# Two token blocks at once in the second of two MLPs behind bucketed attention, and more attention tiles transposed by DMA

## The chip, the cores and the metric

One core of one Trainium2 chip. The metric is the device time of one execution in microseconds (us), as the median of several runs; lower is better.

## The reference

```python
q_bucket, k_bucket = bits of (q @ proj > 0), (k @ proj > 0)      # 6 bits: 64 buckets
scores = where(q_bucket == k_bucket, q @ k.T / 8, -1e9)
attn = softmax(scores) @ v            # 2 batches, 8 heads, 768 tokens, 64 columns
x = attn as 1536 tokens x 512
g = s * relu(x @ w1_in) ** 2 + b;     y = g @ w1_out             # 512 -> 2048 -> 512
h = y @ w2_in; g = h * clip(h + 3, 0, 6) / 6; out = g @ w2_out   # 512 -> 2048 -> 512
```

All inputs are float32 and the output is float32.

## The kernel before, in words

**Tokens.** The 1536 tokens are four blocks ("units") of 384: two per batch. In attention a unit has four pairs of heads, so there are 16 pairs g, and a pair has six slots: two heads by three tiles of 128 queries. A slot is: scores `S` (128 queries by 768 keys, four matmuls, `qk`, L466), the maximum (`smax`, L475), exp with the row sum (`sexp`, L482), a transposition, and after six slots the product with the values (`pv_mm`, L560). The sums' reciprocals are spread over the partitions and multiplied in (`x_scale`, L570), and the result is kept in two fp32r parts, high and low, in X (`x_hi`, `x_lo`). All large matmuls are made of fp32r parts in this way: high x high, high x low, low x high.

**Two ways to transpose.** Pairs g under DMA_FROM (L31) turn a slot with six transposes on TensorE (`turn`, L514) and copy it out of PSUM (`evict`, L519); their product is 24 fp32 matmuls. Pairs from DMA_FROM on split the slot into two fp16 parts (`s_hi` on ScalarE, L493, `s_lo` on VectorE, L498) and transpose it by a DMA from SP's queue (`s_tr`, L508); their values are scaled, split and transposed too (`v_scale` to `v_tr`, L361 to L386), and the product is 36 fp16 matmuls.

**MLPs.** A job (m, j) is MLP m on block j: 32 weight tiles of 128 x 512, the first 16 for `w_in` (a group of 12 matmuls each, 4 row blocks by 3 parts, L648 to L660), the last 16 for `w_out` (four groups accumulate one output tile). After an input group the activation is made in PSUM and split into G (`g_relu` to `g_lo`). When an MLP's weights are met for the first time they come as 64-bit floats (512 KB a tile), are put together as fp32 (`w_exp`, `w_ends`, `w_join`), and stored to a scratch tensor (`w_store`); later jobs fetch the 256 KB tile (`w_fetch`, L628). Each job splits each tile into a high and a low part (`w_hi` L633, `w_lo` L638), on ScalarE, VectorE or GpSimd.

**Room.** X of blocks 2 and 3 is the room of blocks 0 and 1 (L310). PSUM has two score tiles (a third, `Sx`, during the first unit), one bank for the product, and one, later three banks for the MLP groups.

**The order** is not written by hand. Every operation is given to a planner (`Plan`, L37) with its possible engines, cost, due time, needs and buffers; it lays out a list and the kernel is emitted in that order, each engine's queue in order. Due times come from JOBS (L32): per job (m, j, n), where n is the number of attention slots that run beside it. The first unit's 24 slots come first. `gate` (L734) lets a slot start only when the MLP work is near its place, six slots and ten groups ahead at most, and `pull` (L743) lets a group start only when the slots up to six before its place have been begun. Small DMAs go out on SP's or ScalarE's queue as the planner finds room.

Of the kernel before, what the change touches and what calls it, by code (L numbers as in the profile page):

```python
# [19 lines left out]
S = 768  # L20
# [221 lines left out]
def attn_moe_moe2(ctx, tc, qT, kT, vN, vT, cst, w1_in, w1_out, w2_in, w2_out, out):  # L242
# [403 lines left out]
    acc = {}  # L646

    def mm(key, i, j, k):  # L648
        hi, lo = wq[key]["hi"], wq[key]["lo"]
        c = i % 4  # L650
        if i < 16:
            src, k0, nk = X[j], 0, 4
        else:
            src, k0, nk = G[4 * c:4 * c + 4], 4 * c, 16
        if k0 + k == 0:
            acc[key[0]] = ps[ring(("acc", key))].tile([128, 512], F32, tag="mm", name="mm")
        a = acc[key[0]][:, 0:NQ]
        for p, (w, xi) in enumerate(((hi, 0), (hi, 1), (lo, 0))):
            nc.tensor.matmul(out=a, lhsT=w[:, k, :], rhs=src[k][:, xi, :],  # L659
                             start=(k0 + k == 0 and p == 0), stop=(k0 + k == nk - 1 and p == 2))  # L660
        if k == 3:
            acc[key] = a
            del wq[key]
# [3 lines left out]
    def g_relu(m, f, key):  # L667
        h = acc.pop(key)
# [85 lines left out]
    for g in range(NP):  # L754
# [33 lines left out]
        if by_dma(g):  # L788
# [4 lines left out]
            add("TR", t + 8, (1.4, 3.7, 0.3), v_tr, (g,), needs=[("vl", g)], acq=[("v", ("v", g))], gives=[("v", g)], rel=[(("vh", g),)])  # L793
        else:
            add("DMA", t + 4, (0.62, 1.1, 0.8), load_v, (g,), acq=[("v", ("v", g))], gives=[("v", g)])
        for i in range(SPP):
# [10 lines left out]
            if by_dma(g):  # L807
                add("ACT", a + 3.4, 0.8, s_hi, (s,), needs=[("ex", s)], acq=[("P", ("P", s))], gives=[("hi", s)])
                add("DVE", a + 4.3, 0.96, s_lo, (s,), needs=[("hi", s)], gives=[("lo", s)], rel=[(("S", s),)])
                add("TR", a + 5.4, (1.4, 3.7, 0.3), s_tr, (s,), needs=[("lo", s)] + ([("wi", "t", s - 1)] if tq else []), acq=pt,  # L810
# [5 lines left out]
        add("PE", a + 6.0, 3.2 if by_dma(g) else 4.2, pv_mm, (g,), needs=[("pt", SPP * g + i) for i in range(SPP)] + [("v", g)],  # L816
            acq=[("pv", ("pv", g))], gives=[("pv", g)], rel=[(("pt", g, 0),), (("pt", g, 1),), (("v", g),)])
# [8 lines left out]
    def before(k, jn, i):  # L826
        return [(k,) + divmod(32 * jn + i - 1, 32)] if jn + i else []

    for jn, (m, j, n) in enumerate(JOBS):
        t0, dt = M[jn]  # L830
        prev = [("mm", jn - 1, 28 + f // 4) if jn else None for f in range(16)]
        for i in range(32):
            key = (jn, i)
            t = t0 + i * dt
            if jn == first[m]:
                tw = t - 4.0
                add("DMA", tw - 4.0, (0.45, 1.46, 0.8), w_load, (m, i, key), needs=[("pv", 0)] if m == 0 else past(jn, i, AHEAD),
                    acq=[("wr", ("wr", key))], gives=[("wr",) + key])
                add("ACT", tw, 0.68, w_exp, (key,), needs=[("wr",) + key], gives=[("we",) + key])
                add({"ACT": 0.79, "POOL": 0.8, "DVE": 0.46}, tw, 0, w_ends, (key, 0), needs=[("wr",) + key] + before("wi", jn, i),  # L840
                    acq=[("wf", ("wf", key))], gives=[("wd", 0) + key] + [("wi",) + key])
                add("DVE", tw, 0.46, w_ends, (key, 1), needs=[("we",) + key, ("wd", 0) + key], gives=[("wd", 1) + key])
                add("DVE", tw, 0.69, w_join, (key,), needs=[("wd", 1) + key], gives=[("wf",) + key], rel=[(("wr", key),)])
                last = [(("wf", key), 2)]
                add("DMA", tw, (0.45, 0.73, 1.9), w_store, (m, i, key), needs=[("wf",) + key], gives=[("ws", m, i)], rel=last)
            else:
                add("DMA", t - 4.0, (0.45, 0.73, 0.0), w_fetch, (m, i, key), needs=[("ws", m, i)] + past(jn, i, AHEAD) + before("wi", jn, i),
                    acq=[("wf", ("wf", key))], gives=[("wf",) + key, ("wi",) + key])
                last = [(("wf", key),)]
            add({"ACT": 0.62, "DVE": 0.42}, t - 2.0, 0, w_hi, (key,), needs=[("wf",) + key] + before("wh", jn, i), acq=[("wh", ("wh", key))], gives=[("wh",) + key])  # L850
            add({"POOL": 1.3, "DVE": 0.67}, t - 2.0, 0, w_lo, (key,), needs=[("wh",) + key], acq=[("wl", ("wl", key))], gives=[("wl",) + key], rel=last)
            acc_key = ("acc", key if i < 16 else (jn, i - i % 4))
            for k in range(4):
                if i < 16:
                    ins = ("x", j, k) if m == 0 else ("y", j, k)
                else:
                    ins = ("g", jn, 4 * (i % 4) + k)
                head = k == 0 and (i < 16 or i % 4 == 0)
                ins = [ins] + (pull(jn, i) if k == 0 else [])
                add("PE", t + k * dt / 4, MM / 4, mm, (key, i, j, k),  # L860
                    needs=[("wh",) + key, ("wl",) + key] + ins + ([("mk", jn, i, k - 1)] if k else past(jn, i, 1) + (["banks"] if head and (jn or i) else [("R", g) for g in range(4)] if head else [])),
                    acq=[("mm" if jn == 0 and i == 0 else ("mm", "mmx"), acc_key)] if head else [],
                    gives=[("mm", jn, i) if k == 3 else ("mk", jn, i, k)],
                    rel=[(("wh", key),), (("wl", key),)] if k == 3 else [])
            te = t + dt
            if i < 16:
                add("ACT", te, 0.48, g_relu, (m, i, key), needs=[("mm", jn, i)], acq=[("r", ("r", key))], gives=[("gr", jn, i)])
                add("DVE", te + 0.1, 0.6, g_prod, (m, i), needs=[("gr", jn, i)], gives=[("gp", jn, i)], rel=[(("r", key),)])
                add("ACT", te + 0.2, 0.48, g_hi, (m, i), needs=[("gp", jn, i), "G"] + [p for p in prev[i:i + 1] if p],
                    gives=[("gh", jn, i)])  # L870
                add("DVE", te + 0.3, 0.6, g_lo, (m, i), needs=[("gh", jn, i)], gives=[("g", jn, i)], rel=[(acc_key,)])
            elif i % 4 == 3:
                d = (i - 16) // 4
# [80 lines left out]
```

## Time and profile before

| | |
|---|---|
| median of 3 runs | 786.98 us (785.93 to 787.44) |
| profiled execution | 784.16 us |
| its span in the profile | 782.4 us |
| TensorE matmuls busy | 763.2 us, 98% |
| TensorE weight loads, VectorE, ScalarE, GpSimd | 88%, 79%, 60%, 22% |
| mean share of the DMA engines | 66% |

Engines: PE is TensorE's matmuls, PEld its weight loads, DVE VectorE, ACT ScalarE, POOL GpSimd, SP SyncE, whose queue issues most DMAs. In a window's row stand each engine's busy time with its number of instructions, the granted TensorE clock as a share of full speed, the share of the 16 DMA engines and GB/s. A group's row has line, engine, operation, out<-in, shapes, count | busy time, mean ns of one | idle time before it and what ended it. The first matmul of the first MLP starts at 93 us; the jobs' first groups start at 213, 287, 412, 489, 566 and 646 us and so on.

### The profile page before, as it was taken

The numbers are of one execution on the slowest core, as the hardware profiler recorded it, in microseconds if no ns is written. First come the engines' busy times: TensorE is split into PE (matmuls) and PEld (weight loads), VectorE is DVE, ScalarE is ACT, GpSimd is POOL, SyncE is SP. The second block draws the span as 40 slices with busy tenths as digits, with TensorE's granted clock in tenths as the row PEclk, the third lists the DMA queues.
The fourth block names the chain that finished last, engine by engine and source line by source line (L and its number), as shares of the span: only waits on it lengthen the run. The fifth ranks groups of instructions, "written<-read, shape, count | busy, mean of one in ns | idle before, by whom it ended". The sixth has DMA issues, their size and how long they took to land.

```text
span 782.4 us, 13073 instructions
## 1 busy us (share of the span) xinstructions
PE 763.2 (98%) x4620; PEld 688.2 (88%) x4620; DVE 617.8 (79%) x1049; ACT 468.6 (60%) x853; POOL 172.9 (22%) x142
## 2 busy tenths in 40 slices
PE   8888899999999999999999999999999999999998
PEld 4565678989899997877979999999999999999998
DVE  6888788999887679999978866887787758856862
ACT  5777668876575368978867722854377416503710
POOL 4213134332300013452322510521012100001000
PEclk7999999999999999999999999999999999999999
DMA  7378775688644677887998848866785764444441
GB/s 272 97 272 331 267 245 177 207 322 268 224 142 129 234 223 251 263 305 244 338 293 196 252 146 206 225 160 157 187 237 127 200 156 132 124 134 121 132 139 39
DMA packets 105057, 159.93 MB, mean 204 GB/s; under 512 B 50592, under 2 KB 56864, under 8 KB 104992
## 3 DMA queue, kind: packets, MB, share of 16 engines
q1 hardware_dynamic: 104704, 158.89, 66.0%
q8 instruction: 36, 0.59, 0.3%
q14 instruction: 29, 0.24, 0.1%
q10 hardware_dynamic: 288, 0.22, 0.1%
HBM read 115.56 MB, written 32.51 MB: 189 GB/s over the span
## 4 chain that ended last, share of the span: by engine, by line
PE 88%; DVE 4%; ACT 3%; DMA 3%; issue 1%; SPq 0%; DVEq 0%; ACTq 0%
PE mm L659 66%; PE S L471 7%; PE pv L566 7%; PE S L517 5%; DMA wr<-w_in 2%; DVE nx L477 1%; PE S L431 1%; DMA krx<-k_t 1%; ACT P L490 1%; PE S L444 1%; DVE wf L611 1%; PE S L549 0%; DVE K1x L459 0%; DVE wf L620 0%; DVE pt L528 0%
## 5 line engine op out<-in xcount | busy, mean ns | idle before, releaser
L659 PE MATMUL mm<-X,wh 128*128 128x384 f32 x1024 | 264.9, 339 | 0.5 <-DVE G L693 0.4
L659 PE MATMUL mm<-G,wh 128*128 128x384 f32 x1024 | 265.3, 340 | 0.0
L642 POOL TENSOR_TENSOR wl<-wf,wh 128x512 fp32r<-128x512 f32 x84 | 113.5, 1355 | 413.2 <-DVE wh L393 226.4
L659 PEld LDWEIGHTS mm<-X,wh 128*128 128x128 f32 x1024 | 181.5, 188 | 6.7 <-issue 3.7
L659 PEld LDWEIGHTS mm<-G,wh 128*128 128x128 f32 x1024 | 181.7, 188 | 4.6 <-issue 3.3
L659 PE MATMUL mm<-G,wl 128*128 128x384 f32 x512 | 172.4, 337 | 0.0
L659 PE MATMUL mm<-X,wl 128*128 128x384 f32 x512 | 172.0, 336 | 0.0
L642 DVE TENSOR_TENSOR wl<-wf,wh 128x512 fp32r<-128x512 f32 x172 | 120.9, 705 | 12.2 <-ACT wh L390 3.3
L390 ACT ACTIVATE wh<-wf 128x512 fp32r<-128x512 f32 x145 | 90.5, 628 | 47.4 <-PE mm L659 32.5
L477 DVE TENSOR_REDUCE nx<-S 128x1 f32<-128x768 f32 x96 | 90.4, 953 | 21.1 <-PE S L471 20.6
L659 PEld LDWEIGHTS mm<-G,wl 128*128 128x128 f32 x512 | 96.0, 188 | 0.1
L659 PEld LDWEIGHTS mm<-X,wl 128*128 128x128 f32 x512 | 96.1, 188 | 0.0
L393 DVE TENSOR_SCALAR wh<-wf 128x512 fp32r<-128x512 f32 x111 | 47.6, 429 | 52.0 <-PE mm L659 49.2
L490 ACT ACTIVATE P<-S,nx 128x768 f32<-128x768 f32 x72 | 64.7, 901 | 16.4 <-DVE nx L477 15.9
L471 PE MATMUL S<-K,Q 128*128 128x512 f32 (+1 forms) x312 | 69.7, 350 | 1.4 <-DVE pt L528 0.4
L517 PE MATMUL S<-cw,P 128*128 128x128 f32 x432 | 61.0, 281 | 6.9 <-ACT P L490 6.7
L517 PEld LDWEIGHTS S<-cw,P 128*128 128x128 f32 x432 | 51.0, 144 | 15.9 <-ACT P L490 12.1
L471 PEld LDWEIGHTS S<-K,Q 128*128 128x128 f32 x312 | 52.0, 194 | 9.4 <-issue 1.8
L614 POOL TENSOR_SCALAR wf<-wr 128x512 uint16<-128x512 uint16 x36 | 30.9, 857 | 106.6 <-DMA wr<-w_in 29.1
L566 PE MATMUL pv<-pt,v 128*64 128x384 f32 (+1 forms) x384 | 53.4, 429 | 0.1
L620 DVE SCALAR_TENSOR_TENSOR wf<-wr,wf 128x512 int32<-128x512 int32 x64 | 48.1, 755 | 2.4
L611 DVE TENSOR_SCALAR wf<-wr 128x512 uint16<-128x512 uint16 x89 | 46.3, 534 | 4.2 <-ACT wr L602 2.5
(381 smaller groups left out, 820.6 us busy)
## 6 DMA issues: line engine op xcount, KB each, us to landing
wf<-w SPq DMA_DIRECT2D x192, 256.0 KB, 2.7
wr<-w_in SPq DMA_DIRECT2D x32, 512.0 KB, 5.3
w<-wf SPq DMA_DIRECT2D x64, 256.0 KB, 5.5
wr<-w_out SPq DMA_DIRECT2D x32, 512.0 KB, 5.5
K<-ks SPq DMA_DIRECT2D x16, 768.0 KB, 6.6
ks<-K SPq DMA_DIRECT2D x10, 768.0 KB, 7.8
qr<-q_t SPq DMA_DIRECT2D x14, 384.0 KB, 4.4
kr<-k_t SPq DMA_DIRECT2D x6, 768.0 KB, 5.3
```

The costliest lines, as they stand in the source:

```text
L390: nc.scalar.activation(out=out, in_=in_, func=AF.Copy, scale=scale)
L393: e.tensor_scalar(out=out, in0=in_, scalar1=scale, scalar2=None, op0=ALU.mult)
L471: nc.tensor.matmul(out=sp[:, c0:c1], lhsT=queries(g)[a][:, h, 128 * t:128 * t + 128], rhs=keys(g)[a][:, h, c0:c1], start=(a == 0), stop=(a ...
L477: nc.vector.reduce_max(out=nx, in_=sd[s]["sp"][:, 0:S], axis=AX.X, negate=True)
L490: nc.scalar.activation(out=d["p"], in_=d["sp"][:, 0:S], func=AF.Exp, bias=d["nx"], scale=1.0, accum_out=pd[g]["sums"][:, c:c + 1])
L517: nc.tensor.transpose(d["sp"][:, 128 * c:128 * c + 128], d["p"][:, 128 * c:128 * c + 128], ident)
L566: nc.tensor.matmul(out=d["pv"][64 * h:64 * h + 64, 0:NQ], lhsT=d["v"][:, vc, 64 * h:64 * h + 64], rhs=d[h][:, :, pc, :] if by_dma(g) else ...
L611: nc.vector.tensor_scalar(out=f16, in0=r16, scalar1=(13, 0x8000)[half], scalar2=None, op0=(ALU.logical_shift_right, ALU.bitwise_and)[half])
L614: nc.gpsimd.tensor_scalar(out=f16, in0=r16, scalar1=2.0 ** -13, scalar2=2.0 ** -14 - 0.5, op0=ALU.mult, op1=ALU.add)
L620: nc.vector.scalar_tensor_tensor(out=wf, in0=wq[key]["raw"][:, :, 1], scalar=3, in1=wf, op0=ALU.logical_shift_left, op1=ALU.bitwise_or)
L642: e.tensor_tensor(out=lo.rearrange("p a b -> p (a b)"), in0=d["wf"], in1=d["hi"].rearrange("p a b -> p (a b)").bitcast(F32), op=ALU.subtract)
L659: nc.tensor.matmul(out=a, lhsT=w[:, k, :], rhs=src[k][:, xi, :], start=(k0 + k == 0 and p == 0), stop=(k0 + k == nk - 1 and p == 2))
```

## The change

- DMA_FROM goes from 12 to 9: pairs 9, 10 and 11 are transposed by DMA as pairs 12 to 15 are.
- JOBS: the second MLP runs on blocks 0 and 1 together, and on 2 and 3 together. Each of its 32 weight tiles is fetched and split once for two groups, one per block. As G holds 16 tiles, it goes by halves of the features: eight input tiles and eight output tiles for half 0, then half 1. The outputs of half 0 go to a scratch tensor and are fetched and added after half 1.
- Order of jobs: before (MLP, block) 00, 01, 10, 11, 02, 12, 03, 13 with 24, 10, 8, 10, 10, 10, 0, 0 slots; now 00, 01, 1 on 0 and 1, 02, 03, 1 on 2 and 3 with 24, 12, 18, 18, 0, 0 slots.
- X of block 2 gets its own room; block 3 uses that of block 0.
- The product of the first four pairs is emitted in three parts (`PV_PARTS`), the third score tile is used for two more slots (`XT`), and in the first two further groups of a first-MLP job a group's last row block may follow the next groups' first ones (`EASE`).
- The planner's cost of a transposing DMA goes from 3.7 to 2.2 us.

```diff
-WARM, PTX, DMA_FROM = 12, 2, 12
+WARM, PTX, DMA_FROM = 12, 2, 9
+PV_PARTS, EASE = 3, 3
-JOBS = ((0, 0, 24), (0, 1, 10), (1, 0, 8), (1, 1, 10), (0, 2, 10), (1, 2, 10), (0, 3, 0), (1, 3, 0))
+JOBS = ((0, (0,), 24), (0, (1,), 12), (1, (0, 1), 18), (0, (2,), 18), (0, (3,), 0), (1, (2, 3), 0))
...
-        X.append([p.tile([128, 2, NQ], F32R, name=f"X1{k}") for k in range(4)])
-        X.extend(X[0:2])
+        X.extend([p.tile([128, 2, NQ], F32R, name=f"X{u}{k}") for k in range(4)] for u in (1, 2))
+        X.append(X[0])
...
-    def pv_mm(g):
+    def pv_mm(g, part):
         d = pd[g]
-        d["pv"] = ps_v.tile([128, 512], F32, tag="pv", name="pv")
-        for c in range(NC):
+        if part == 0:
+            d["pv"] = ps_v.tile([128, 512], F32, tag="pv", name="pv")
+        n = NC // parts(g)
+        for c in range(n * part, n * part + n):
...
+    oscr = [[dr_p.tile([128, NQ], F32, name=f"o{j}{d}") for d in range(4)] for j in range(4)]
+    def mm(n, k):
+        V, src, j, c0, nk, name = group[n]
+        hi, lo = wq[V]["hi"], wq[V]["lo"]
+        if c0 + k == 0:
+            acc[name] = ps[ring(("acc", name))].tile([128, 512], F32, tag="mm", name="mm")
+        a = acc[name][:, 0:NQ]
         for p, (w, xi) in enumerate(((hi, 0), (hi, 1), (lo, 0))):
+            nc.tensor.matmul(out=a, lhsT=w[:, k, :], rhs=(X[j] if src is None else G[src:])[k][:, xi, :],
+                             start=(c0 + k == 0 and p == 0), stop=(c0 + k == nk - 1 and p == 2))
...
+    def o_keep(j, d):
+        queue[0].dma_start(out=oscr[j][d], in_=od.pop((j, d)))
+    def o_fetch(j, d):
+        od[j, d] = o_tile()
+        queue[0].dma_start(out=od[j, d], in_=oscr[j][d])
+    def o_add(j, d, name):
+        o = od[j, d]
+        nc.vector.scalar_tensor_tensor(out=o, in0=acc.pop(name)[:, 0:NQ], scalar=1.0 / 6.0, in1=o, op0=ALU.mult, op1=ALU.add)
...
+        for x in range(halves):
+            for i in [fs * x + f for f in range(fs)] + [16 + 4 * d + cs * x + c for d in range(4) for c in range(cs)]:
+                for e, j in enumerate(blocks):
...
+                    group.append((len(visits), None if i < 16 else fs * e + 4 * (c - cs * x), j, 0 if i < 16 else 4 * (c - cs * x),
+                                  4 if i < 16 else 4 * cs, name))
...
-    XT = SPU - 4
+    XT = SPU - 2
...
-            add("TR", t + 8, (1.4, 3.7, 0.3), v_tr, (g,), needs=[("vl", g)], acq=[("v", ("v", g))], gives=[("v", g)], rel=[(("vh", g),)])
+            add("TR", t + 8, (1.4, 2.2, 0.0), v_tr, (g,), needs=[("vl", g)], acq=[("v", ("v", g))], gives=[("v", g)], rel=[(("vh", g),)])
...
-        add("ACT", a + 11.0, 0.48, x_hi, (g,), needs=[("xs", g)] + (["G"] if u else []) + ([("mm", jobs[1, u - 2], 15)] if u > 1 else []), gives=[("xh", g)])
+        add("ACT", a + 11.0, 0.48, x_hi, (g,), needs=[("xs", g)] + (["G"] if u else []) + (past(y_last[0]) if u == 3 else []), gives=[("xh", g)])
```

## Rows read from the trace of the kernel before

**Rows 1.** The page's head: busy time by engine, and VectorE's busy tenths in 40 slices.
```profile
PE 763.2 (98%) x4620; PEld 688.2 (88%) x4620; DVE 617.8 (79%) x1049; ACT 468.6 (60%) x853; POOL 172.9 (22%) x142
DVE  6888788999887679999978866887787758856862
```

**Rows 2.** Windows by job from 93 us on, and a stretch late in the last jobs.
```profile
93.00:213.00 120.00, 119.58 (x759) 102.85 (x758) 108.80 (x177) 85.40 (x158) 41.76 (x35) 1.00 0.73 244
213.00:287.00 74.00, 74.00 (x431) 73.43 (x430) 56.33 (x94) 41.21 (x76) 5.64 (x6) 1.00 0.56 182
287.00:412.00 125.00, 123.56 (x777) 103.03 (x776) 113.95 (x192) 100.29 (x178) 42.99 (x37) 1.00 0.83 281
412.00:489.00 77.00, 77.00 (x465) 74.47 (x464) 56.40 (x104) 39.94 (x78) 19.43 (x14) 1.00 0.76 199
489.00:566.00 77.00, 77.00 (x466) 74.41 (x465) 61.64 (x110) 43.02 (x82) 19.93 (x15) 1.00 0.71 184
566.00:646.00 80.00, 79.61 (x494) 75.99 (x493) 57.86 (x108) 42.81 (x82) 11.59 (x9) 1.00 0.70 178
...
650.00:750.00 100.00, 100.00 (x578) 100.00 (x578) 74.89 (x134) 48.46 (x92) 5.18 (x4) 1.00 0.45 127
```

**Rows 3.** TensorE's longest wait: us in total, times, longest.
```profile
PE S L517 <- ACT P L490: 6.7, 8, 2.1
```

**Rows 4.** Timeline of TensorE around one slot's transposes and two products: start, us.
```profile
120.32 0.88 PE L517 MATMUL S<-cw,P 128*128 128x128 f32 x6
120.95 0.60 PE L659 MATMUL mm<-X,wh 128*128 128x384 f32 x2
...
164.43 4.09 PE L566 MATMUL pv<-pt,v 128*64 128x384 f32 x24
168.45 0.61 PE L659 MATMUL mm<-G,wh 128*128 128x384 f32 x2
...
457.20 3.12 PE L566 MATMUL pv<-pt,v 128*64 128x384 f16 x36
460.24 0.62 PE L659 MATMUL mm<-G,wh 128*128 128x384 f32 x2
```

**Rows 5.** Groups of VectorE: the weights' splits, and the low part of a slot.
```profile
L642 DVE TENSOR_TENSOR wl<-wf,wh 128x512 fp32r<-128x512 f32 x172 | 120.9, 705 | 12.2 <-ACT wh L390 3.3 <-DVE wh L393 0.5 <-ACT G L685 0.3
L393 DVE TENSOR_SCALAR wh<-wf 128x512 fp32r<-128x512 f32 x111 | 47.6, 429 | 52.0 <-PE mm L659 49.2 <-POOL wl L642 1.7 <-issue 0.4
L500 DVE TENSOR_TENSOR P<-S,P 128x768 f16<-128x768 f32 x24 | 22.9, 954 | 2.3 <-ACT P L496 2.0
```

**Rows 6.** DMA of 489 to 566 us, of 650 to 750 us, and SP's issue of transposes.
```profile
q1 hardware_dynamic: 19293, 14.07, 71.2%
wf<-w SPq DMA_DIRECT2D x32, 256.0 KB, 3.1
K<-ks SPq DMA_DIRECT2D x2, 768.0 KB, 5.7
v<-v_t SPq DMA_DIRECT2D x1, 384.0 KB, 3.0
out<-o__5545 SPq DMA_DIRECT2D x1, 192.0 KB, 1.9
pt<-P SPq DMA_TRANSPOSE x8, 4.5
v<-P SPq DMA_TRANSPOSE x1, 3.7
...
wf<-w SPq DMA_DIRECT2D x49, 256.0 KB, 2.6
...
L512 SPq DMA_TRANSPOSE pt<-P x24: 1280/1752/2750, 407.4 to 628.8; - x24
```

**Rows 7.** Windows of 25 us around the second MLP's first job.
```profile
375.00:400.00 25.00, 25.00 (x162) 21.16 (x161) 22.29 (x40) 17.43 (x31) 5.80 (x5) 1.00 0.93 340
400.00:425.00 25.00, 25.00 (x150) 24.07 (x150) 20.01 (x36) 16.97 (x32) 7.04 (x5) 1.00 0.90 227
```

More of the change, by code (lines that the diff above doesn't have):

```diff
@@ L558, in r_copy, with parts @@
         pd[g]["R"] = R
-    def pv_mm(g):
+    def parts(g):
+        return PV_PARTS if g < 4 else 1
+    def pv_mm(g, part):
         d = pd[g]
-        d["pv"] = ps_v.tile([128, 512], F32, tag="pv", name="pv")
-        for c in range(NC):
+        if part == 0:
+            d["pv"] = ps_v.tile([128, 512], F32, tag="pv", name="pv")
+        n = NC // parts(g)
+        for c in range(n * part, n * part + n):
             for n, (vc, pc) in enumerate(((c, c), (c, NC + c), (NC + c, c)) if by_dma(g) else ((c, c),)):
@@ L644, in w_lo, with g_relu @@
         d["lo"] = lo
[L646 to L657, printed above, removed]
-        for p, (w, xi) in enumerate(((hi, 0), (hi, 1), (lo, 0))):
[L659 to L663, printed above, removed]
+    acc, od, group = {}, {}, []
+    oscr = [[dr_p.tile([128, NQ], F32, name=f"o{j}{d}") for d in range(4)] for j in range(4)]
[5 more added lines that the diff above has]
+        a = acc[name][:, 0:NQ]
+        for p, (w, xi) in enumerate(((hi, 0), (hi, 1), (lo, 0))):
+            nc.tensor.matmul(out=a, lhsT=w[:, k, :], rhs=(X[j] if src is None else G[src:])[k][:, xi, :],
+                             start=(c0 + k == 0 and p == 0), stop=(c0 + k == nk - 1 and p == 2))
     gt = {}
-    def g_relu(m, f, key):
-        h = acc.pop(key)
+    def g_relu(m, f, name):
+        h = acc.pop(name)[:, 0:NQ]
         r = ev_p.tile([128, NQ], F32, tag="r", name="r_")
@@ L716, in attn_moe_moe2 @@
     add = plan.add
+    visits, work, heads = [], [], []
+    for jn, (m, blocks, n) in enumerate(JOBS):
+        halves = len(blocks)
+        fs, cs = 16 // halves, 4 // halves
+        heads.append(len(work))
+        for x in range(halves):
+            for i in [fs * x + f for f in range(fs)] + [16 + 4 * d + cs * x + c for d in range(4) for c in range(cs)]:
+                for e, j in enumerate(blocks):
+                    d, c = divmod(i - 16, 4)
+                    name = ("in", jn, i, j) if i < 16 else ("out", jn, x, d, j)
+                    group.append((len(visits), None if i < 16 else fs * e + 4 * (c - cs * x), j, 0 if i < 16 else 4 * (c - cs * x),
+                                  4 if i < 16 else 4 * cs, name))
+                    work.append((jn, x, e))
+                visits.append((jn, i, len(group) - 1))
+    heads.append(len(work))
     A = [T0 + PACE0 * s for s in range(SPU)]
@@ L720, in attn_moe_moe2, with past @@
     M = []
-    for m, j, n in JOBS:
-        dt = MM + n * SL / 32
+    for jn, (m, blocks, n) in enumerate(JOBS):
+        ng = heads[jn + 1] - heads[jn]
+        dt = MM + n * SL / ng
         M.append((tj, dt))
-        A += [tj - 12 + (x + 0.5) * 32 * dt / n for x in range(n)]
-        tj += 32 * dt
-    jobs = {(m, j): n for n, (m, j, _) in enumerate(JOBS)}
+        A += [tj - 12 + (x + 0.5) * ng * dt / n for x in range(n)]
+        tj += ng * dt
     first = {m: min(n for n, job in enumerate(JOBS) if job[0] == m) for m in range(2)}
-    def past(jn, i, n):
-        x = 32 * jn + i - n
-        return [("mm",) + divmod(x, 32)] if x >= 0 else []
+    def past(n):
+        return [("mm", n)] if n >= 0 else []
     def gate(s):
@@ L740, in gate, with pull @@
             jn += 1
-        return past(jn, int(32 * s / JOBS[jn][2]), SLACK) if s >= 0 else []
-    def pull(jn, i):
-        s = SPU + sum(job[2] for job in JOBS[:jn]) + JOBS[jn][2] * i // 32 - PULL
+        return past(heads[jn] + int((heads[jn + 1] - heads[jn]) * s / JOBS[jn][2]) - SLACK) if s >= 0 else []
+    def pull(n):
+        jn = work[n][0]
+        s = SPU + sum(job[2] for job in JOBS[:jn]) + JOBS[jn][2] * (n - heads[jn]) // (heads[jn + 1] - heads[jn]) - PULL
         return [("qk", s)] if s >= SPU and JOBS[jn][2] else []
+    y_last = {j: max(n for n, g in enumerate(group) if g[1] is None and g[2] == j and JOBS[work[n][0]][0] == 1) for j in range(4)}
     add("PE", -80.0, 0.22 * WARM, warm, (WARM,), acq=[("pv", "w")], rel=[("w",)], soon=-80.0)
-    XT = SPU - 4
+    XT = SPU - 2
     add("PE", A[SPU - 1] + 0.1, 0.0, mm_banks, (),
@@ L809, in attn_moe_moe2 @@
                 add("DVE", a + 4.3, 0.96, s_lo, (s,), needs=[("hi", s)], gives=[("lo", s)], rel=[(("S", s),)])
[L810 removed]
+                add("TR", a + 5.4, (1.4, 2.2, 0.0), s_tr, (s,), needs=[("lo", s)] + ([("wi", "t", s - 1)] if tq else []), acq=pt,
                     gives=[("pt", s), ("wi", "t", s)], rel=[(("P", s),)])
@@ L815, in attn_moe_moe2 @@
                 acq=pt, gives=[("pt", s)], rel=[(("S", s),)])
-        add("PE", a + 6.0, 3.2 if by_dma(g) else 4.2, pv_mm, (g,), needs=[("pt", SPP * g + i) for i in range(SPP)] + [("v", g)],
-            acq=[("pv", ("pv", g))], gives=[("pv", g)], rel=[(("pt", g, 0),), (("pt", g, 1),), (("v", g),)])
+        for x in range(parts(g)):
+            last = x == parts(g) - 1
+            add("PE", a + 6.0, 3.2 if by_dma(g) else 4.03 / parts(g) + 0.17, pv_mm, (g, x),
+                needs=[("pt", SPP * g + i) for i in range(SPP)] + [("v", g)] + ([("pvp", g, x - 1)] if x else []),
+                acq=[] if x else [("pv", ("pv", g))], gives=[("pv", g) if last else ("pvp", g, x)],
+                rel=[(("pt", g, 0),), (("pt", g, 1),), (("v", g),)] if last else [])
         add("DVE", a + 3.6, 0.36, recip, (g,), needs=[("ex", SPP * g + i) for i in range(SPP)], gives=[("rc", g)])
@@ L829, in attn_moe_moe2 @@
-    for jn, (m, j, n) in enumerate(JOBS):
-        t0, dt = M[jn]
[L831 to L845, printed above, removed]
-            else:
[L847 to L873, printed above, removed]
-                if m == 0:
-                    add("ACT", te, 0.48, y_hi, (j, d, key), needs=[("mm", jn, i)], gives=[("yh", jn, d)])
-                    add("DVE", te, 0.55, y_lo, (j, d, key), needs=[("yh", jn, d)], gives=[("y", j, d)], rel=[(acc_key,)])
-                else:
-                    add("ACT", te, 0.48, o_copy, (j, d, key), needs=[("mm", jn, i)], acq=[("o", ("o", key))], gives=[("o", jn, d)], rel=[(acc_key,)])
-                    add("DMA", te, (0.45, 0.55, 1.5), o_store, (j, d, key), needs=[("o", jn, d)], gives=[("os", jn, d)], rel=[(("o", key),)])
@@ new lines, in before @@
+    def before(k, V):
+        return [(k, V - 1)] if V else []
+    for V, (jn, i, n) in enumerate(visits):
+        m, blocks = JOBS[jn][:2]
+        t = M[jn][0] + (n - len(blocks) + 1 - heads[jn]) * M[jn][1]
+        ahead = past(visits[V - AHEAD][2]) if V >= AHEAD else []
+        if jn == first[m]:
+            tw = t - 4.0
+            add("DMA", tw - 4.0, (0.45, 1.46, 0.8), w_load, (m, i, V), needs=[("pv", 0)] if m == 0 else ahead,
+                acq=[("wr", ("wr", V))], gives=[("wr", V)])
+            add("ACT", tw, 0.68, w_exp, (V,), needs=[("wr", V)], gives=[("we", V)])
+            add({"ACT": 0.79, "POOL": 0.8, "DVE": 0.46}, tw, 0, w_ends, (V, 0), needs=[("wr", V)] + before("wi", V),
+                acq=[("wf", ("wf", V))], gives=[("wd", 0, V), ("wi", V)])
+            add("DVE", tw, 0.46, w_ends, (V, 1), needs=[("we", V), ("wd", 0, V)], gives=[("wd", 1, V)])
+            add("DVE", tw, 0.69, w_join, (V,), needs=[("wd", 1, V)], gives=[("wf", V)], rel=[(("wr", V),)])
+            last = [(("wf", V), 2)]
+            add("DMA", tw, (0.45, 0.73, 1.9), w_store, (m, i, V), needs=[("wf", V)], gives=[("ws", m, i)], rel=last)
+        else:
+            add("DMA", t - 4.0, (0.45, 0.73, 0.0), w_fetch, (m, i, V), needs=[("ws", m, i)] + ahead + before("wi", V),
+                acq=[("wf", ("wf", V))], gives=[("wf", V), ("wi", V)])
+            last = [(("wf", V),)]
+        add({"ACT": 0.62, "DVE": 0.42}, t - 2.0, 0, w_hi, (V,), needs=[("wf", V)] + before("wh", V), acq=[("wh", ("wh", V))], gives=[("wh", V)])
+        add({"POOL": 1.3, "DVE": 0.67}, t - 2.0, 0, w_lo, (V,), needs=[("wh", V)], acq=[("wl", ("wl", V))], gives=[("wl", V)], rel=last)
@@ new lines, in attn_moe_moe2 @@
+    g_read = {}
+    for n, (V, src, j, c0, nk, name) in enumerate(group):
+        jn, x, e = work[n]
+        m, blocks = JOBS[jn][:2]
+        i = visits[V][1]
+        d = (i - 16) // 4
+        t0, dt = M[jn]
+        t = t0 + (n - heads[jn]) * dt
+        if i < 16:
+            f = i if len(blocks) == 1 else 8 * e + i % 8
+            ins = [("x" if m == 0 else "y", j, k) for k in range(4)]
+        else:
+            ins = [("g", jn, x, src + k) for k in range(4)]
+        for k in range(4):
+            need = [ins[k]] + (pull(n) if k == 0 else [])
+            if k == 3 or 0 < n - heads[jn] < EASE and m == 0:
+                need.append(("mk", n - 1, 2) if k == 0 else ("mk", n, k - 1))
+                if k == 3:
+                    need += past(n - 1)
+            elif k:
+                need.append(("mk", n, k - 1))
+            else:
+                need += past(n - 1)
+            head = c0 + k == 0
+            if head:
+                need += ["banks"] if n else [("R", g) for g in range(4)]
+            add("PE", t + k * dt / 4, MM / 4, mm, (n, k), needs=[("wh", V), ("wl", V)] + need,
+                acq=[("mm" if n == 0 else ("mm", "mmx"), ("acc", name))] if head else [],
+                gives=[("mm", n) if k == 3 else ("mk", n, k)],
+                rel=[(("wh", V), len(blocks)), (("wl", V), len(blocks))] if k == 3 else [])
+        te = t + dt
+        if i < 16:
+            add("ACT", te, 0.48, g_relu, (m, f, name), needs=[("mm", n)], acq=[("r", ("r", n))], gives=[("gr", n)])
+            add("DVE", te + 0.1, 0.6, g_prod, (m, f), needs=[("gr", n)], gives=[("gp", n)], rel=[(("r", n),)])
+            add("ACT", te + 0.2, 0.48, g_hi, (m, f), needs=[("gp", n), "G"] + past(g_read.get(f, -1)), gives=[("gh", n)])
+            add("DVE", te + 0.3, 0.6, g_lo, (m, f), needs=[("gh", n)], gives=[("g", jn, x, f)], rel=[(("acc", name),)])
+            continue
+        for k in range(4):
+            g_read[src + k] = n
+        if c0 + 4 < nk:
+            continue
+        bank = [(("acc", name),)]
+        if m == 0:
+            add("ACT", te, 0.48, y_hi, (j, d, name), needs=[("mm", n)], gives=[("yh", n)])
+            add("DVE", te, 0.55, y_lo, (j, d, name), needs=[("yh", n)], gives=[("y", j, d)], rel=bank)
+            continue
+        if x == 0:
+            add("ACT", te, 0.48, o_copy, (j, d, name), needs=[("mm", n)], acq=[("o", ("o", n))], gives=[("o", n)], rel=bank)
+        else:
+            add("DMA", t - 6.0, (0.45, 0.55, 0.8), o_fetch, (j, d), needs=[("ok", j, d)] + past(n - 4), acq=[("o", ("o", n))], gives=[("of", n)])
+            add("DVE", te, 0.6, o_add, (j, d, name), needs=[("mm", n), ("of", n)], gives=[("o", n)], rel=bank)
+        if x == len(blocks) - 1:
+            add("DMA", te, (0.45, 0.55, 1.5), o_store, (j, d), needs=[("o", n)], gives=[("os", n)], rel=[(("o", n),)])
+        else:
+            add("DMA", te, (0.45, 0.55, 1.5), o_keep, (j, d), needs=[("o", n)], gives=[("ok", j, d)], rel=[(("o", n),)])
```

24 lines of the change are left out of this document (12 added, 12 removed).

## The prediction, made before the change was run

> **What bounds the kernel now.** I read the page's head first, then the stretches job by job, then TensorE's waits. The head shows TensorE busy for 98% of the span [rows 1]; a pipelined matmul hides small waits in such a number, so the stretches matter more. In each of them from 93 us on PE's busy time nearly equals the length, at full clock [rows 2]: 119.6 of 120, 74 of 74, 123.6 of 125, 77 of 77, 77 of 77, 79.6 of 80. The largest wait in PE's list comes to 6.7 us in the whole run [rows 3]. A pure stretch fixes the price of the MLP work: 578 matmuls in 100 us, 0.173 us each, 2.08 us for a group of twelve [rows 2]. So from 93 us on the time is the sum of what TensorE is given, and PE work that is taken away shortens the run one for one, unless another resource then falls behind. The two that could are in the same table: in 287 to 412 us DVE is busy 114 of 125 us and the DMA engines 83%, while elsewhere between 213 and 646 us DVE is at 72 to 80% and DMA at 56 to 76% [rows 2].
>
> **Pairs 9, 10, 11 turned by DMA.** Each loses its six slots' transposes on PE, and its product is made from fp16 parts instead of fp32. The six transposes of one slot delay TensorE by at least 0.63 us (from its first start at 120.32 to the next matmul's at 120.95) and by at most the 0.88 us of their own row [rows 4]. I take 0.72, near the lower end, since the first matmul behind it starts while the last transposes run, but is itself longer. 18 x 0.72 = 13.0 us, bounds 11.3 and 15.8. The product costs 4.02 us from its start to the next matmul (164.43 to 168.45) against 3.04 with 36 fp16 matmuls (457.20 to 460.24) [rows 4]: 3 x 0.98 = 2.9 us. Together **-15.9 us** (-14.2 to -18.7). All three pairs run in stretches where PE is full, so all of it lies on the path.
>
> Added beside PE: on DVE 18 low parts of 0.95 us, and per pair a low part and a maximum over as many values, taken at the same [rows 5]: 24 x 0.95, some 23 us; and 21 DMA transposes, six per pair and one for its values. Their price comes from 489 to 566 us: the queue took 71.2% of 77 us, 54.8 us, for 32 weight tiles, two key tiles, one of values, one output and nine transposes [rows 6]. The weight tile costs 0.85 us: in 650 to 750 us 49 of them and about five outputs (three quarters of a tile) filled 45% of 100 us [rows 2, 6]. By bytes a key tile is three of these, values one and a half. 54.8 - 27.2 - 5.1 - 1.3 - 0.6 = 20.6 us, 2.3 us a transpose, so 48 us more DMA. On SP's queue an issue takes 1.75 us [rows 6], 37 us in 350: the weight fetches behind it are sent for up to five tiles ahead, 0 unless the queue is short (below). The evictions that these slots no longer need I count for nothing; ACT and DVE did them beside PE.
>
> **Second MLP on two blocks.** PE work: none saved, none added; the same 128 groups in another order. 64 weight fetches go (54 us of DMA), with 64 splits, of which DVE did 111 of 256 high parts at 0.43 and 172 of 256 low parts at 0.71 [rows 5]: 64 x 0.66 = 42 us. Added are 16 stores and 16 fetches of partial sums (32 x 0.64 = 20 us of DMA on SP's or ACT's queue) and 16 more evictions, half of all by DVE at about 0.6 us. PE covers these; without that cover the 16 would cost 10 us. The last one adds 0.1 us to the end. On SP's queue a fetch of a partial sum waits for its store; behind it stand weight fetches, and the store is eight visits, some 17 us or more, old: 0. Accumulators: two stay open over four groups, the third bank takes the next; an eviction has 2.08 us for some 0.7. Cost 0, at worst 16 x 0.5 = 8 us.
>
> **Third block in its own room.** The copies of its x no longer wait for the second MLP of block 0; nothing waited there, 0. But unit 3 now waits for the room of block 0 until the second half's input groups have read it, 48 groups into a job of 64. Behind that wait stand the one bank of the product and, behind it, the next pair's product.
>
> **First 93 us.** Products in thirds let scores and transposes pass between. Four products of the fp32 kind, 4.02 us [rows 4], stand there; at best each frees two thirds, 2.7 us, -10.7; if the chain goes through DVE anyway, nothing, and eight more breaks cost at most 8 x 0.1 = 0.8. DVE is at 60 to 80% of its slices there [rows 1], so I take **-4**. The wider third score bank and the eased job heads are in this: no wait of PE for an x tile comes near the largest on the list [rows 3].
>
> **What is late next.** Take 213 to 646 us, jobs 1 to 5, 433 us [rows 2]. In the new order one second-MLP job of 32 groups (66.6 us) leaves it for the tail, and 15.9 us vanish: 350 us of PE. DMA there: 41.4 + 103.8 + 58.5 + 54.7 + 56.0 = 314 us now; without two sets of fetches and four outputs (54 and 3), with 48 of transposes and 10 of partial sums, 316 us. So the queue goes from 73% to 90% of the stretch. DVE goes from 346 us to at most 346 + 23 + 5 - 42 = 332, at most 95%, and what leaves with the job, and the low parts that POOL (under a quarter busy [rows 1]) can take, brings it under the 91% that it now holds in 287 to 412. The tightest part is the last, after block 0's room is free: 16 groups of the second MLP, 32 of the third block and 18 slots. A DMA-turned slot costs PE (77 - 66.6) / 8 = 1.3 us [rows 2, 6], so 100 + 23 = 123 us of PE. DMA: 48 transposes + 27 weights + 20 first loads and stores of eight weight tiles + 15 keys + 8 queries and values + 10 sums and outputs = 128 us. That is over the stretch. Early loads can move some 8 us out, cost 0; at the 93% that the queue held at most over 25 us with PE full [rows 7], 128 / 0.93 - 123 = 15. I take **+6**, in the lower half because two stretches of 25 us at 93 and 90% left PE at 25.00 [rows 7].
>
> **Sum.** -15.9 - 4 + 6 = -13.9. The profiled execution took 784.16 us (span 782.4), so 770.3; the median of the runs shown is 2.8 above it: **773 us**.
>
> A figure against my price of a transpose: the Trainium skill, "DMA: Bandwidth & Descriptors", section "Latency and other measured facts", gives DMA transposes an effective 261 GB/s; a tile of 393 KB would take an estimated 1.5 us, the shortage and the +6 would fall away, and the sum would be 767. The trace disagrees with 2.3 us.
>
> **Rivals.**
> (a) No shortage and a better start. Early loads cover the queue's peak and the thirds bring 8 us: 784.2 - 15.9 - 8 + 2.8 = 763. For it: the same 316 us of DMA lie in both orders. Against: the 128 of 123 us. 17%.
> (b) Slower: the DMA queue becomes the bound of jobs 1 to 3. SP issues in order and waits for buffers, so it may not exceed the 83% mean of the densest stretch [rows 2]: 316 / 0.83 = 381 us against 350, +31, hence 784.2 - 15.9 - 4 + 31 + 2.8 = 798. It decides from where the reachable share falls below 316 / (350 + 20) = 85%. Against: 93 and 90% with PE full [rows 7]. 13%.
> (c) The removed PE work lay where TensorE wasn't the bound. The pairs lie around 287 to 412 us, where PEld is busy only 103 of 125 us and DVE 114 [rows 2]; if DVE sets the pace there, the 15.9 us bring nothing: 784.2 - 4 + 6 + 2.8 = 789, or 783 without the shortage. Against: PE's idle time of 1.4 us there. 10%.
> By the Trainium skill, "Trainium Kernel Development and Optimization", section "Best Practices", one judges by the busy share of weight loads and not of matmuls, which speaks for (c); the trace bears it out little, since the fp32 products and transposes there load few weights for their time.
> (d) The planner's new order has a flaw that I don't see, or the parts don't do what they say: 3%.
>
> **How the numbers follow.** My case has 57%, 773 with 764 to 783 of its own (start 0 to -8, shortage 0 to +15, pairs as bounded). The range 760 to 790 takes in (a) and (c) and leaves out most of (b) and a little of (a), under 2 in 10. A measurement here tells 0.2%, 1.6 us, from no change: 785.4 to 788.6 is the same. Faster: my case, (a), half of (c) and a third of (d), 0.80; same: the other half of (c), whose times lie on both sides, and a third of (d), 0.06; slower: (b) and the rest of (d), 0.14.
>
> **What would show it.** Right: 108 fewer PE transposes, 21 more DMA transposes, PE full in every stretch from the first MLP group on, the DMA share near 90% over the two middle jobs, and a few us of PE idle before scores or products that wait for a transposed tile in the last stretch before attention ends. Wrong: PE idle at the head of the fourth first-MLP job of more than 10 us (then (b)); waits of scores or weights on DVE (then (c)); a first MLP group no earlier than 93 us (then the start's term).

## The result, and the profile after

The changed kernel took 767.03 us (766.58 to 767.53, 4 runs) against 786.63 us of the kernel before (785.93 to 787.44, 4 runs): ratio 0.9751, 95% interval 0.9734 to 0.9768. That is 19.6 us less where 13.9 were forecast; it lies in the range of 760 to 790. The profiled execution's span fell from 782.4 to 764.7 us, by 17.7.

The head of the page after answers to [rows 1]; PE's and the other busy times, and the queue:

```profile
span 764.7 us, 12760 instructions
...
PE 746.4 (98%) x4548; PEld 675.4 (88%) x4548; DVE 588.1 (77%) x1014; ACT 454.8 (59%) x827; POOL 168.8 (22%) x147
...
DMA packets 133376, 157.70 MB, mean 206 GB/s; under 512 B 83008, under 2 KB 93376, under 8 KB 133312
...
q1 hardware_dynamic: 133024, 156.66, 69.5%
```

TensorE is as full as before, with 16.8 us less of busy time; DVE lost 30 us of work. The windows of the new jobs, which answer to [rows 2]: first MLP on block 0, on block 1, second MLP on both, first MLP on block 2, on block 3, second MLP on both:

```profile
89.30:215.70 126.40, 126.37 (x812) 109.04 (x812) 111.25 (x186) 97.51 (x176) 41.82 (x38) 1.00 0.73 256
215.70:305.90 90.20, 88.79 (x540) 81.07 (x537) 75.38 (x131) 59.22 (x109) 30.37 (x24) 1.00 0.82 225
305.90:478.40 172.50, 168.77 (x1046) 156.51 (x1045) 152.65 (x276) 109.64 (x201) 51.33 (x48) 1.00 0.99 271
478.40:561.20 82.80, 82.80 (x515) 78.41 (x514) 66.27 (x121) 47.70 (x92) 18.15 (x15) 1.00 0.82 199
561.20:627.80 66.60, 66.60 (x386) 66.60 (x386) 47.66 (x84) 26.79 (x52) 3.87 (x3) 1.00 0.44 127
627.80:764.70 136.90, 133.36 (x769) 133.04 (x767) 62.63 (x112) 48.00 (x91) 1.29 (x1) 1.00 0.27 83
```

PE is busy nearly all of each window at full clock, and the DMA share is 0.99 over the 172 us of the two-block job.

To compare kernels whose jobs differ, I price what TensorE did in each stretch: 0.1735 us for an MLP matmul, 0.70 for a slot's scores, 0.70 for its six transposes, 4.2 and 3.2 for the two kinds of product, about 1 to 2 us a pair for the codes. What is left of a stretch I call lost. These are estimates from the spacing of the matmuls in the trace; over the pure stretches they leave 0.1 us. The price of the transposes is a little high: where a slot's six stand between MLP matmuls, 31 of 36 such places before the change and 20 of 21 after it show 0.66 us.

| us | PE work | lost before the first MLP group | lost in the jobs beside attention | lost in the tail |
|---|---|---|---|---|
| before | 746.4 | 24.4 | 8.2 | 3.4 |
| after | 730.8 | 18.6 | 11.7 | 3.7 |

So the 17.7 us are 15.6 of PE work, 5.8 of the start, and 3.8 given back later, most of it in the two-block job (7.5 us lost). At 0.66 a slot the 15.6 would be 14.9 and the 3.8 would be 3.1. (That the PE work before equals the busy time on the page after, 746.4, is chance.)

### The profile page after: what moved, and what is told of

Same layout as the page of the kernel before. It is cut to its first block, busy times and chain, and to the rows that moved or that the text cites. A ratio compares the mean times of both kernels' runs of the same rounds, so it can differ in the third digit from the quotient of the medians.

```text
span 764.7 us, 12760 instructions
## 1 busy us (share of the span) xinstructions
PE 746.4 (98%) x4548; PEld 675.4 (88%) x4548; DVE 588.1 (77%) x1014; ACT 454.8 (59%) x827; POOL 168.8 (22%) x147
## 4 chain that ended last, share of the span: by engine, by line
PE 89%; DVE 6%; DMA 2%; ACT 1%; issue 1%; ACTq 0%; DVEq 0%; SPq 0%
PE mm L664 68%; PE S L473 8%; PE pv L573 7%; PE S L519 4%; DVE nx L479 1%; PE S L433 1%; PE S L446 1%; DMA v<-P 1%; DMA wr<-w_in 1%; DMA cw<-cst 1%; PE S L551 1%; DVE wf L627 0%; DVE P L502 0%; DVE wf L618 0%; DVE mm L680 0%
## 5 line engine op out<-in xcount | busy, mean ns | idle before, releaser
L649 POOL TENSOR_TENSOR wl<-wf,wh 128x512 fp32r<-128x512 f32 x80 | 105.8, 1325 | 261.5 <-ACT wh L392 151.0
L392 ACT ACTIVATE wh<-wf 128x512 fp32r<-128x512 f32 x113 | 71.1, 632 | 40.1 <-PE mm L664 19.9
L649 DVE TENSOR_TENSOR wl<-wf,wh 128x512 fp32r<-128x512 f32 x112 | 78.2, 698 | 7.4 <-ACT wh L392 2.6
L395 DVE TENSOR_SCALAR wh<-wf 128x512 fp32r<-128x512 f32 x79 | 34.3, 434 | 49.4 <-PE mm L664 47.8
L621 POOL TENSOR_SCALAR wf<-wr 128x512 uint16<-128x512 uint16 x49 | 42.7, 871 | 123.7 <-DMA wr<-w_in 30.3
L492 ACT ACTIVATE P<-S,nx 128x768 f32<-128x768 f32 x54 | 48.7, 904 | 11.9 <-DVE nx L479 11.3
L492 ACT ACTIVATE S<-S,nx 128x768 f32<-128x768 f32 x42 | 36.7, 875 | 26.6 <-DVE nx L481 19.5
L573 PE MATMUL pv<-pt,v 128*64 128x384 f16 (+1 forms) x420 | 51.3, 393 | 0.0
L609 ACT ACTIVATE wr<-wr 128x512 f32<-128x512 f32 x64 | 43.0, 683 | 10.5 <-DMA wr<-w_out 7.1
L519 PE MATMUL S<-cw,P 128*128 128x128 f32 x324 | 45.3, 279 | 2.2 <-ACT P L492 2.2
```

The lines of the kernel that those rows point to most:

```text
L392: nc.scalar.activation(out=out, in_=in_, func=AF.Copy, scale=scale)
L395: e.tensor_scalar(out=out, in0=in_, scalar1=scale, scalar2=None, op0=ALU.mult)
L492: nc.scalar.activation(out=d["p"], in_=d["sp"][:, 0:S], func=AF.Exp, bias=d["nx"], scale=1.0, accum_out=pd[g]["sums"][:, c:c + 1])
L519: nc.tensor.transpose(d["sp"][:, 128 * c:128 * c + 128], d["p"][:, 128 * c:128 * c + 128], ident)
L609: nc.scalar.activation(out=a, in_=a, func=AF.Copy, scale=2.0 ** -112)
L621: nc.gpsimd.tensor_scalar(out=f16, in0=r16, scalar1=2.0 ** -13, scalar2=2.0 ** -14 - 0.5, op0=ALU.mult, op1=ALU.add)
```

## The experiments

Each ratio is to the kernel before, measured beside it on the same chip; "from 9" means pairs from 9 on turned by DMA.

**Pairs 9 to 11 back on TensorE.**

```diff
-WARM, PTX, DMA_FROM = 12, 2, 9
+WARM, PTX, DMA_FROM = 12, 2, 12
```

> Changed kernel, but pairs 9 to 11 turned on TensorE again; the second MLP stays on two blocks, the start stays. Theory (TensorE's sum): the 15.7 us of PE work come back, less at most the 3 to 4 us that PE now loses more in the two-block job, since the DMA queue gets 48 us less: 779 to 783 us. Rival 1 (the gain is the second MLP's halved fetches and splits): most of the gain stays, 768 to 772.

778.61 us, ratio 0.9915 (0.9891 to 0.9940). PE work is back at 746.4 us, and 2.9 us less are lost in the start and the jobs than in the changed kernel. With the rest of the change in place the pairs are worth 11.6 us of its 19.6. The time lies a little under the theory's window and far from rival 1's: only some 7 us of the gain stay.

**One block per second-MLP job.**

```diff
-JOBS = ((0, (0,), 24), (0, (1,), 12), (1, (0, 1), 18), (0, (2,), 18), (0, (3,), 0), (1, (2, 3), 0))
+JOBS = ((0, (0,), 24), (0, (1,), 10), (1, (0,), 8), (1, (1,), 10), (0, (2,), 10), (1, (2,), 10), (0, (3,), 0), (1, (3,), 0))
```

> Changed kernel with the second MLP one block at a time and the slots per job of before; pairs 9 to 11 by DMA and the new start stay. Theory: same PE work, and 10 slots per 32 groups leave the DMA queue at 70 to 95% in each job: 764 to 769 us. Rival 1: without the halved fetches the gain is lost, 780 to 787. Rival 2 (the two-block job is only there to make room for the transposes in the queue): between them, 772 to 778.

788.22 us, ratio 1.0026 (1.0013 to 1.0040): the whole gain is gone, with PE work still at 730.8 us. My theory fell here; the number lies 1 us above rival 1's window. I call this one the one-block kernel.

**The kernel before, with pairs from 9 alone.**

```diff
-WARM, PTX, DMA_FROM = 12, 2, 12
+WARM, PTX, DMA_FROM = 12, 2, 9
```

(and the planner's cost of a transposing DMA as in the change)

> Kernel before with pairs 9 to 11 by DMA and the planner's new cost of a transposing DMA, nothing else. Theory: 15.9 us of PE work less, nothing else moves: 769 to 773 us. Rival 1: no gain without the two-block job, 783 to 790.

787.26 us, ratio 1.0028 (1.0013 to 1.0044). Again 15.6 us of PE work less and no time, as rival 1 had it. Both kernels lose it in one place, the first job of the second MLP, where its weights are met for the first time. This is that job's window in the one-block kernel, then two shorter ones inside it, to be held against the row of 287 to 412 us in [rows 2]:

```profile
287.90:400.40 112.50, 97.23 (x551) 85.96 (x548) 106.18 (x176) 83.64 (x149) 40.59 (x31) 0.94 1.00 291
310.00:330.00 20.00, 12.76 (x60) 11.38 (x60) 19.65 (x28) 15.27 (x28) 11.94 (x8) 0.91 0.98 295
350.00:370.00 20.00, 16.39 (x87) 15.68 (x86) 19.46 (x32) 15.51 (x26) 10.83 (x9) 0.91 1.01 322
```

PE has 97 of 112 us, and by the prices above 24.6 us are lost there (18.9 in the kernel before from 9). DVE is busy 94% of it, 98% where PE starves most; the DMA share is 1.00; and the granted clock is 0.94, so some of the work there runs slower as well. The job also holds less: the planner put 12 attention slots beside it, where the kernel before has 21, and more beside the later jobs. Two resources are full, so the next two runs take work from one at a time, in the same planned order.

**The one-block kernel, with less DMA.** The second MLP's weights are not stored; its later jobs read the first MLP's stored tiles, so the second MLP is computed with other weights there.

```diff
-        queue[0].dma_start(out=wscr[m][i], in_=wdone.pop(key))
+        done = wdone.pop(key)
+        if m == 0:
+            queue[0].dma_start(out=wscr[m][i], in_=done)
...
-        queue[0].dma_start(out=wf, in_=wscr[m][i])
+        queue[0].dma_start(out=wf, in_=wscr[0][i])
```

> The kernel with one block per second-MLP job and pairs 9 to 11 by DMA (788 us, 24.6 us lost by PE in the first second-MLP job, DMA share 1.00, DVE 94% there). The second MLP's weights are not stored, its later jobs read the first MLP's stored tiles: 27 us of DMA less in that job, DVE's and PE's work and the planned order unchanged. Theory D (the DMA queue is what binds that job): most of the loss goes, 765 to 772 us. Theory V (DVE binds it): 784 to 789.

787.74 us, ratio 1.0027 (1.0016 to 1.0038): nothing.

**The one-block kernel, with less DVE.** The stores are back, and the join is left out for the second MLP, whose weights then lack the bits that it puts in.

```diff
-        nc.vector.scalar_tensor_tensor(out=wf, in0=wq[key]["raw"][:, :, 1], scalar=3, in1=wf, op0=ALU.logical_shift_left,
-                                       op1=ALU.bitwise_or)
+        if JOBS[visits[key][0]][0] == 0:
+            nc.vector.scalar_tensor_tensor(out=wf, in0=wq[key]["raw"][:, :, 1], scalar=3, in1=wf, op0=ALU.logical_shift_left,
+                                           op1=ALU.bitwise_or)
```

> The same kernel, its stores kept, but the joining of the second MLP's weights from two words left out: 32 DVE instructions of 0.74 us, 24 us of DVE, less in that job, the DMA and the planned order unchanged. Theory D: 785 to 789 us. Theory V: 766 to 774.

776.86 us, ratio 0.9886 (0.9866 to 0.9907): 11.4 us less than with the join, nearer to theory V's window than to D's and in neither. The job itself takes 112.5 us in the one-block kernel, 113.2 without the stores and 102.8 without the join. The same stretch, 287 to 400 us, in the one-block kernel, without the stores, and without the join, one row from each of the three profiles:

```profile
287.00:400.00 113.00, 97.73 (x554) 85.72 (x553) 106.68 (x177) 83.98 (x149) 41.31 (x32) 0.94 1.00 292
```

```profile
287.00:400.00 113.00, 99.32 (x546) 88.38 (x547) 105.66 (x176) 83.51 (x150) 42.36 (x32) 0.91 0.88 228
```

```profile
287.00:400.00 113.00, 103.31 (x623) 90.61 (x625) 93.19 (x164) 91.89 (x164) 43.70 (x34) 0.98 1.03 320
```

Without the stores the DMA share falls from 1.00 to 0.88 and DVE and PE do about the same work as before. Without the join DVE falls by 13 us, PE does 69 matmuls more in the same time, and the DMA share rises above 1 (the last 10 us of that row belong to the next job). So the join on DVE holds that job back, and the queue's work doesn't. The gain is half of the 24 us taken out, and 14.9 us are still lost; ACT is then at 92 of 113 us. What binds next was not tried. Nor does the run tell the join's time on DVE from the buffer that it holds: there are three for the raw weights, the join frees one, and in the one-block kernel SP's queue waits 22.4 us, in 15 waits, for joins before it can issue the next load. Without the join 4.6 us of it are left, behind the instruction before it. The changed kernel's two-block job has the same wait, 24.6 us in 14, and there it costs little (below).

**The changed kernel, with less DMA and with less DVE.** The same two edits as above, in the changed kernel.

> The changed kernel with the second MLP's weights not stored (later job reads the first MLP's tiles): 27 us of DMA less in the two-block job, where the share is 0.99 and PE loses 7.5 us. Theory D: 3 to 6 us of the loss go, 761 to 764. Theory V (DVE or plain latency): 766 to 768.

768.71 us, ratio 0.9772 (0.9748 to 0.9797). No gain, and theory V's side; the two-block job's window answers to the one at 305.90 us above:

```profile
310.50:482.80 172.30, 168.76 (x1045) 156.51 (x1045) 151.48 (x276) 109.12 (x201) 51.06 (x48) 1.00 0.86 224
```

The share went from 0.99 to 0.86, the job from 172.5 to 172.3 us. A queue at 0.99 costs nothing that shows here.

> The changed kernel with the joining of the second MLP's weights from two words left out: 24 us of DVE less in the two-block job (172 us, DVE 88%, DMA 0.99, PE loses 7.5 us), DMA and the planned order unchanged. Theory V (DVE is what still costs PE there): 3 to 7 us less, 760 to 764 us. Theory D: 766 to 769.

764.96 us, ratio 0.9741 (0.9715 to 0.9766), which the interval doesn't tell from the changed kernel's 0.9751; it lies between the two windows. In the profile the job takes 170.1 us instead of 172.5 and loses 5.0 instead of 7.5. So about a third of what is lost there goes with the join. Neither less DMA nor less DVE moved the rest, and it stays open.

**The old start**, then one part of it at a time.

```diff
-PV_PARTS, EASE = 3, 3
+PV_PARTS, EASE = 1, 0
...
-    XT = SPU - 2
+    XT = SPU - 4
```

> Changed kernel with the product in one part, the third score tile for 20 slots and the job heads in strict order. Theory: the 5.8 us that PE idles less before the first MLP group come back, 771 to 774 us. Rival: the start is bound by DVE and the thirds bring nothing, 766 to 769.

778.46 us, ratio 0.9909 (0.9893 to 0.9924): 11.4 us, more than the 5.8 expected. The first MLP group starts at 92.6 us, as before the change, but 6.9 us are then lost in the first job, where the changed kernel loses none.

> The changed kernel with the product of the first four pairs in one part; the third score tile's two more slots and the eased heads stay. Theory: the thirds carry the start, so the 5 us by which PE idles less before the first MLP group come back, 771 to 775 us. Rival: the other two edits carry it, 766 to 769.

(PV_PARTS = 1 alone.) 778.91 us, ratio 0.9908 (0.9887 to 0.9930). The first group starts at 94.3 us: the thirds carry the start. But the first job loses 8.6 us too.

> The changed kernel with the groups at the head of a first-MLP job in strict order again, thirds and third score tile as changed. Theory (thirds carry the start): 766 to 769 us. Rival (the eased heads save a stall in the first job, where the kernel with all of the old start lost 6.9 us after its first MLP group): 771 to 776.

(EASE = 0 alone.) 777.60 us, ratio 0.9909 (0.9875 to 0.9943). The first group starts at 88.7 us, so the eased heads don't touch the start; 8 us more are lost over the next three jobs. All three times lie above both windows of their expectations. The thirds or the eased heads, taken out alone, cost what all three edits cost together (the third score tile wasn't tried alone), so they can't be summed: the planner lays out another order for the whole kernel each time. How much of these 11 us is the edit and how much that order is open.

**Two more orders.**

```diff
-WARM, PTX, DMA_FROM = 12, 2, 9
+WARM, PTX, DMA_FROM = 12, 2, 8
```

> The changed kernel with pair 8 by DMA too: 5.2 us of PE work less, 16 us of DMA more, in the jobs where the share is 0.82 to 0.99. Theory D: the queue pays back about what PE saves, 764 to 769. Theory V (the queue has room left): 761 to 763.

772.59 us, ratio 0.9834 (0.9812 to 0.9856), worse than either expectation. PE work falls to 725.6 us, but the first job takes 133 us for 124 of PE work; its window:

```profile
88.20:221.20 133.00, 127.76 (x791) 108.16 (x790) 124.68 (x199) 101.32 (x185) 45.31 (x41) 1.00 0.83 263
```

DVE is at 94% there, as in the one-block kernel's bad job, against 88% in the changed kernel's first job, and the queue at 0.83. It fits a bound by DVE but wasn't tested, and the order is another one as well.

```diff
-JOBS = ((0, (0,), 24), (0, (1,), 12), (1, (0, 1), 18), (0, (2,), 18), (0, (3,), 0), (1, (2, 3), 0))
+JOBS = ((0, (0,), 24), (0, (1,), 13), (1, (0, 1), 18), (0, (2,), 17), (0, (3,), 0), (1, (2, 3), 0))
```

> The changed kernel with one slot moved from the third block's job to block 1's (13 and 17 instead of 12 and 18). Theory V (only the two-block job, with DVE at 88%, still costs PE some us, and it keeps its 18 slots): no difference that can be told, 765 to 769 us. Rival (the last stretch before attention ends is the tight one, as predicted): 762 to 765.

769.46 us, ratio 0.9788 (0.9769 to 0.9808): nothing won, perhaps 2 us lost, just above the theory's window. The rival's gain didn't come. Of the variants that compute the same result, none beat the changed kernel.

## Why the prediction was right, and where it was wrong

**The pairs (-15.9).** The term was right as PE work: 15.6 us by prices (14.9 with 0.66 us for a slot's transposes, where the prediction took 0.72), 108 transposes fewer, 21 more DMA transposes (49 after 28). The sentence "all three pairs run in stretches where PE is full, so all of it lies on the path" was wrong as a reason. With one block per second-MLP job the same PE work is gone and no time with it (1.0026 and 1.0028). In the job from 287 us PE and DVE were both nearly full [rows 2]; the pairs took from the one and gave to the other. With two blocks the pairs do pay, 11.6 us.

**Second MLP on two blocks ("PE covers these", cost 0).** This is the step that failed. I counted 42 us of DVE work saved, used it only to keep DVE's mean over the stretch under 95%, and gave it no price in the sum. In the orders that the planner made, it is the condition for the pairs: the first pass over the second MLP's weights costs DVE the same work per tile, but with two blocks there are two groups of PE work beside each tile, and DVE fell from 94% of a 112 us job to 88% of a 172 us job. With the pairs in place it is worth 21 us (788.22 against 767.03). Rival (c), DVE setting the pace around 287 to 412 us, is what happens without it; for the whole change (c) was wrong. That the join's 24 us bring 11.4 back in the one-block kernel, and about 2 in the changed one, is the test of that. It accounts for some half of the 21 us; the other half stays open, since the two kernels' orders differ as well. One reason given against (c) doesn't hold either: from 287 to 412 us the products do load few weights, 6.5 us of loads in some 16 us, but the 20 slots' transposes load 13.8 us in an estimated 13.

**What is late next (+6, the queue).** The demand was right: 0.82 x 90.2 + 0.99 x 172.5 + 0.82 x 82.8 = 313 us of DMA in 345.5 us, 90%, where 316 of 350 stood. The conclusion was wrong. I took 93% as the most that the queue had held [rows 7] for about the most that it can hold; it ran at 0.99 for 172 us, and taking 13% of its work out changed nothing. So the shortage isn't there, and rival (b), for which it "may not exceed the 83% mean of the densest stretch", falls with it. Nor did TensorE wait for transposed tiles in the last stretch before attention ends, a sign that I had named: it is busy for all of the 82.80 us there. What the jobs do lose, 3.5 us more than before, is mostly in the two-block job, where less DMA didn't bring it back.

**The start (-4).** The mechanism is seen: the product's thirds run between scores, and the first MLP group starts 3.7 us earlier although 2 us more of PE work lie ahead of it. The size was under: 5.8 us. How much of it is the thirds' is not settled: without them the first group starts at 94.3 us, but in another order. The thirds of the first products, among the longest pieces of the chain of waits after, of eight matmuls each where [rows 4] has 24 in one piece:

```profile
32.80 1.44 PE pv L573 x8
34.24 0.90 PE S L473 x4
36.50 1.44 PE pv L573 x8
37.94 0.90 PE S L473 x4
38.84 1.31 PE S L519 x12
40.15 1.44 PE pv L573 x8
```

**The sum.** -15.6 - 5.8 + 3.8 against -15.9 - 4 + 6, so the right sign and a size 4 us short in the profile, by two terms that erred the same way. That it came so near is in part luck: the +6 was for a shortage that isn't there, and the 3.8 in its place is another loss; and the -15.9 came true only beside an edit that the sum gave nothing. The head of the fourth first-MLP job, which I had named for (b), shows no wait: 66.60 of 66.60 us from 561.20 on.

## What to carry to other kernels

Work taken off a full engine pays only if what it is handed to has room in that very stretch: sum every engine per stretch, for the new order and not for the old. When two resources are both full in a stretch, their shares don't tell which binds; take work from one at a time, in an unchanged order, and see. Where a planner lays out the whole order, an edit taken out alone can cost as much as all of them, so compare kernels of one order where that can be had.

## What the runs showed of the hardware

**A DMA share of 0.99 is no bound by itself.** It stood for 172 us beside a PE that was busy for 168.8 of them, and the share's fall to 0.86 moved the job by 0.2 us. Nor is 1.00 a ceiling of this measure: it read 1.03 over 113 us without the join.

**A VectorE instruction can wait out a GpSimd one.** The join's median is 0.69 us, but in the one-block kernel one took 3.89. VectorE, then GpSimd, from 324 us on:

```profile
324.36 0.45 DVE L618 TENSOR_SCALAR wf<-wr 128x512 uint16<-128x512 uint16 x1
324.92 3.89 DVE L627 SCALAR_TENSOR_TENSOR wf<-wr,wf 128x512 int32<-128x512 int32 x1
328.73 0.55 DVE L680 SCALAR_TENSOR_TENSOR mm<-r__3649,mm 128x384 f32<-128x384 f32 x1
...
324.79 3.46 POOL L402 TENSOR_TENSOR K<-kr,K 64x1536 fp32r<-64x1536 f32 x1 [1.77 <-ACT K L392]
```

GpSimd's subtraction began 0.13 us earlier and ended at 328.25; the join ended 0.56 us after it. Spans on GpSimd are rough in this profile, but the pattern holds over the one-block kernel: each of its 13 joins that took over 0.80 us began while a GpSimd instruction was running. So part of DVE's busy time in a crowded job is waiting, and an operation moved to GpSimd can still cost DVE time. The Trainium skill, "SBUF — State Buffer", section "Who interferes with whom", says that the two engines share a pair of ports under an exclusive lock, and that a VectorE instruction with two inputs in SBUF contends with a GpSimd instruction that reads SBUF. The join has two such inputs, and these rows agree. In the one-block kernel's bad job 27 joins have a mean of 0.92 us, an estimated 6 us above the median in all; how much of the lost 24.6 us this makes wasn't tried.

**The clock falls with the stalls.** In the same job the granted clock had a mean of 0.94. Two windows of the one-block kernel, next to each other:

```profile
320.00:324.00 4.00, 0.93 (x4) 0.60 (x4) 3.93 (x8) 2.99 (x5) 2.04 (x2) 0.95 0.98 230
324.00:327.00 3.00, 2.87 (x9) 2.90 (x10) 2.90 (x3) 2.97 (x6) 2.21 (x1) 0.50 1.06 381
```

PE had been busy 0.93 of 4 us; when its work came it ran at the lower of its two levels, 1.2 GHz, nine matmuls in 3 us where [rows 2] has 17. A stall there costs more than its own length.
